# A two-layer MLP behind a recurrent scan: weight conversion with one POOL instruction less, and a scan whose decay is written straight into an operand

## The chip, the cores and the metric

One core of a Trainium2 chip runs the whole program. The metric is the device time of one execution in microseconds (us), taken in separate runs; the profile is one more execution, recorded by the hardware. The engines are TensorE (PE; its weight loads are PEld), VectorE (DVE), ScalarE (ACT), GpSimd (POOL) and SyncE (SP), which issues nearly all DMAs. Each engine takes its instructions strictly in the order written down for it and waits on semaphores for the others.

## What is computed

A linear recurrence over 768 time steps for 4 batches of 8 heads of width 40, and then two gated MLPs on the 3072 resulting rows of 320 (cut to what matters):

```
y[t] = r[t] @ state
Sa = state @ a[t]
state = state * w[t] - outer(Sa, b[t]) + outer(v[t], k[t])
...
h = x @ w_in;  x = (max(h, 0) + alpha * min(h, 0)) @ w_out
x = (silu(x @ w_gate) * (x @ w_val)) @ w_out2
```

The MLP weights come as 8-byte floats: w_in 320x2048, w_out 2048x320, w_gate and w_val 320x1536, w_out2 1536x320.

## The kernel before, in words

**The scan.** Time is cut into blocks of 128 steps (six, counted by m) and each block into two segments of 64. For each block, `prep_a` and `prep_b` (L491, L524) form decay products (Wx, rest), the matrices AN and kbt and their products on PE; `inverse(m)` (L586) inverts all triangular 32x32 pieces of a block by 31 elimination steps, on DVE and, for block 0, partly on POOL (L617, L625), and ends with two DVE transposes, the second at L631; two rounds of small matmuls (L639, L658) complete it. Then `seq(i, ch)` (L675) runs one batch of one block; two channels ch run side by side, each with one PSUM bank (tag s0 or s1) that all its steps share. A seq has two scan steps c. A step starts with `decay` (L695: the state ST times Wx, DVE, L697), copies the decayed state into halves of the operand gs (DVE, L713; POOL fills the other halves from v at L706), transposes the state on PE (sp, L718), copies that to s on ACT (L720), and then makes the products zp (L725, from gs), pp, gp and yp. At its end DVE adds the new part to the state (L775) and writes the output piece (L779).

**The conversion.** `conv` (L196) loads one 128-row piece of 8-byte weights as pairs of 32-bit words (tile raw, two buffers) and `narrow` (L173) makes fp32 of it. Three DVE bit instructions fold the exponent and join sign, high and low bits: L179 (mask and shift the high word, into wy), L180 (add the sign, into wz), L181 (add three low bits, into wy). ACT then writes the absolute value of the high word, read as fp32, into wz (L182); POOL compares it with a least value (L188) and multiplies the 0 or 1 into wy's number (L189), so that too small numbers become 0. `split` (L192) makes a rounded head on ACT (L193) and the rest on POOL (L194). There is one buffer of wy (YB = 1) and there are two of wz (ZB = 2). 32 pieces of the first MLP and 12 of the second go back to DRAM (tensor wd) and are fetched again as wt; 24 more of the second are converted late and directly into place (`direct`, L921), and in every other one of those DVE does comparison and product in one instruction (L184). An issue rule keeps POOL's instruction at L188 behind the last elimination step that POOL was given.

**The order.** `drive` (L127) draws from generators (preparations, inverse, the two scan channels, conversions, the first MLP `mlp1` of the block before) at given rates, each with a priority, and a scheduler then writes a fixed order for each engine. So a changed instruction can move all others. The first MLP of block m - 1 runs beside the scan of block m; after the last block's first MLP the second MLP runs alone (L960 on), from 885 us.

Of the kernel before, what the change touches and what calls it, by code (L numbers as in the profile page):

```python
# [7 lines left out]
F32 = mybir.dt.float32  # L8
F32R = mybir.dt.float32r
U32 = mybir.dt.uint32  # L10
ACTF = mybir.ActivationFunctionType
ALU = mybir.AluOpType
# [27 lines left out]
ZB = 2  # L40
GD0 = 0
GD1 = 0
GD2 = 0
BGS = 0
# [7 lines left out]
YB = 1  # L52
# [17 lines left out]
L = 64  # L70
# [5 lines left out]
def kernel(  # L76
# [15 lines left out]
    nc = tc.nc  # L92
# [78 lines left out]
    LEAST = 1.125 * 2.0 ** -15  # L171

    def narrow(pool, raw, dve=0):  # L173
        whi, wlo = raw[..., 1], raw[..., 0]
        sh = list(whi.shape)
        y = pool.tile(sh, U32, tag="wy", name="wy", bufs=YB)
        z = pool.tile(sh, U32, tag="wz", name="wz", bufs=ZB)
        f = z.bitcast(F32)
        nc.vector.tensor_scalar(y, whi, 0x07FFFFFF, 3, ALU.bitwise_and, ALU.logical_shift_left)  # L179
        nc.vector.scalar_tensor_tensor(z, whi, 0xC0000000, y, ALU.bitwise_and, ALU.bitwise_or)  # L180
        nc.vector.scalar_tensor_tensor(y, wlo, 29, z, ALU.logical_shift_right, ALU.bitwise_or)  # L181
        nc.scalar.activation(out=f, in_=whi.bitcast(F32), func=ACTF.Abs)  # L182
        if dve:
            nc.vector.scalar_tensor_tensor(f, f, LEAST, y.bitcast(F32), ALU.is_ge, ALU.mult)  # L184
            return f
        gate = tc.issue_after(mark["pool"].ins) if "pool" in mark else nullcontext()
        with gate:
            nc.gpsimd.tensor_scalar(f, f, LEAST, None, ALU.is_ge)  # L188
        nc.gpsimd.tensor_tensor(out=f, in0=f, in1=y.bitcast(F32), op=ALU.mult)  # L189
# [6 lines left out]
    def conv(stage, idx, src, f, kind, into=None, dve=None):  # L196
# [10 lines left out]
        w32 = narrow(stage, raw, (GD0 <= idx < GD1 or idx < 2 * K1 and GD2 and idx % GD2 == 0) if dve is None else dve)  # L207
# [467 lines left out]
    def seq(i, ch, own=None):  # L675
# [19 lines left out]
        def decay(c):  # L695
            std = st[:, :, 0:D].rearrange("q (a j) d -> q a j d", j=2)
            nc.vector.tensor_tensor(  # L697
                out=std, in0=std, in1=wv_all[:, :, :, c, L:L + 1].to_broadcast([128, NP // 2, 2, D]), op=ALU.mult
            )

        decay(0)
        for c in range(CPB):
            cs = slice(c * L, c * L + L)
            gs = (gs_x if i < B and c == 0 and BGS else gs_p).tile([128, NP, 2, L + D], F32, tag="gs", name="gs")
# [7 lines left out]
            for h, pr in ((0, lo), (1, hi)):  # L712
                nc.vector.tensor_copy(  # L713
                    out=gs[pr, h::2, :, L:L + D], in_=st[pr, :, 0:D].rearrange("q (a j) d -> q a j d", j=2)
                )
# [60 lines left out]
            if c < CPB - 1:  # L776
                decay(c + 1)
# [272 lines left out]
```

## Time and profile before

| | us |
|---|---|
| three runs | 1284.64, 1289.05, 1291.42 (median 1289.05) |
| profiled execution, its own time | 1285.88 |
| its span | 1284.2 |
| PE busy | 1107.7 (86% of the span) |
| DVE busy | 797.8 (62%) |
| ACT busy | 594.4 (46%) |
| POOL busy | 378.7 (29%) |
| chain of work that ended last | PE 47%, DVE 17%, DMA 10%, ACT 6%, POOL 3% |
| granted PE clock, mean | 0.942 |

Busy shares are means over stages that differ: in the first tenth of the span DVE is busy 90% and more and PE a third, in the last third it is the other way. A wait is put down to the engine whose signal came last.

### The profile page before, as it was taken

The numbers are of one execution on the slowest core, as the hardware profiler recorded it, in microseconds if no ns is written. First come the engines' busy times: TensorE is split into PE (matmuls) and PEld (weight loads), VectorE is DVE, ScalarE is ACT, GpSimd is POOL, SyncE is SP. The second block draws the span as 40 slices with busy tenths as digits, with TensorE's granted clock in tenths as the row PEclk, the third lists the DMA queues.
The fourth block names the chain that finished last, engine by engine and source line by source line (L and its number), as shares of the span: only waits on it lengthen the run. The fifth ranks groups of instructions, "written<-read, shape, count | busy, mean of one in ns | idle before, by whom it ended". The sixth has DMA issues, their size and how long they took to land.

```text
span 1284.2 us, 24671 instructions
## 1 busy us (share of the span) xinstructions
PE 1107.7 (86%) x9056; PEld 933.6 (73%) x9056; DVE 797.8 (62%) x1725; ACT 594.4 (46%) x1463; POOL 378.7 (29%) x580
## 2 busy tenths in 40 slices
PE   3531778878898998989799989999999999999998
PEld 3431667766677786878677766777888888888887
DVE  6999778899669748975767447657532323232222
ACT  4741666644764575475465344435332323232222
POOL 9786666655320221232046004324200000000000
PEclk9765789989999998999999999999999999999999
DMA  5321368777545444564558567986210101000000
GB/s 156 123 66 46 125 197 277 262 241 227 179 129 174 138 127 142 150 191 117 154 175 255 152 205 248 302 292 205 66 46 1 45 1 36 2 11 11 11 11 21
DMA packets 94215, 170.70 MB, mean 133 GB/s; under 512 B 12944, under 2 KB 42896, under 8 KB 94096
## 3 DMA queue, kind: packets, MB, share of 16 engines
q1 hardware_dynamic: 85936, 165.20, 40.7%
q10 hardware_dynamic: 8160, 3.93, 1.1%
q8 instruction: 72, 1.18, 0.4%
q14 instruction: 47, 0.39, 0.1%
HBM read 141.30 MB, written 27.79 MB: 132 GB/s over the span
## 4 chain that ended last, share of the span: by engine, by line
PE 47%; DVE 17%; DMA 10%; ACT 6%; issue 4%; POOL 3%; SPq 1%; ACTq 0%; DVEq 0%; POOLq 0%
PE pg L238 10%; PE pv L238 10%; PE u L238 6%; DMA wt<-wd 4%; PE o L971 3%; PE o L970 3%; PE o L972 3%; DVE la L625 2%; DVE g L278 2%; DVE tmp L617 2%; PE mnp L543 2%; DMA xd<-pv 2%; PE gp L752 1%; DVE gl L194 1%; DVE wz L180 1%
## 5 line engine op out<-in xcount | busy, mean ns | idle before, releaser
L193 ACT CAST gh<-g 128x512 fp32r<-128x512 f32 (+1 forms) x176 | 105.8, 601 | 170.2 <-DVE g L986 121.4
L986 DVE TENSOR_TENSOR g<-pv,sg 128x512 f32<-128x512 f32 x72 | 49.8, 692 | 216.2 <-PE pv L238 215.3
L194 DVE TENSOR_TENSOR gl<-g,gh 128x512 fp32r<-128x512 f32 (+1 forms) x176 | 123.9, 704 | 76.5 <-ACT gh L193 75.7
L238 PE MATMUL u<-xh,wt 128*128 128x512 f32 (+1 forms) x416 | 148.6, 401 | 25.7 <-DVE g L278 18.4
L278 DVE SCALAR_TENSOR_TENSOR g<-g,neg,u 128x512 f32<-128x512 f32 (+1 forms) x104 | 72.8, 700 | 71.7 <-ACT g L277 71.3
L238 PEld LDWEIGHTS u<-xh,wt 128*128 128x128 f32 x416 | 79.1, 193 | 50.7 <-DVE g L278 26.6
L543 PE MATMUL mnp<-AN,kbt 128*128 128x128 f32 x384 | 66.9, 336 | 51.7 <-DVE AN L518 42.6
L984 ACT ACTIVATE sg<-pg 128x512 f32<-128x512 f32 x72 | 42.9, 598 | 134.9 <-PE pg L238 134.9
L188 POOL TENSOR_SCALAR wz<-wz 128x384 f32<-128x384 f32 (+1 forms) x56 | 67.5, 1206 | 123.0 <-ACT wz L182 60.4
L543 PEld LDWEIGHTS mnp<-AN,kbt 128*128 128x128 f32 x384 | 61.4, 243 | 56.5 <-issue 26.1
L238 PE MATMUL pg<-xh,w 128*128 128x512 f32 x288 | 101.8, 394 | 0.2 <-ACT sg L984 0.2
L238 PE MATMUL pv<-xh,w 128*128 128x512 f32 x288 | 100.5, 389 | 0.0
L277 ACT ACTIVATE g<-u 128x512 f32<-128x512 f32 (+1 forms) x104 | 58.7, 564 | 78.0 <-PE u L238 61.2
L971 PE MATMUL o<-w,gh 128*128 128x320 f32 x288 | 87.7, 309 | 0.0
L970 PE MATMUL o<-w,gh 128*128 128x320 f32 x288 | 87.2, 308 | 0.0
L625 DVE TENSOR_TENSOR la<-la,tmp 128x120 f32<-128x120 f32 (+37 forms) x304 | 84.7, 306 | 1.6
L244 PE MATMUL d<-gl,wt 128*128 128x512 f32 (+1 forms) x208 | 82.6, 400 | 3.0 <-DVE gl L194 2.8
L706 POOL COPY gs<-raw_v 64x160 f32<-64x160 f32 x96 | 37.7, 393 | 160.0 <-PE yp L767 56.3
L617 DVE TENSOR_TENSOR tmp<-la 128x120 f32<-128x120 f32 (+37 forms) x304 | 82.1, 298 | 1.3
L557 POOL TENSOR_SCALAR_AFFINE_SELECT AN<-AN 64x256 f32<-64x256 f32 x96 | 52.1, 543 | 103.1 <-ACT AN L556 65.9
L238 PE MATMUL u<-xl,wt 128*128 128x512 f32 (+1 forms) x208 | 80.7, 388 | 0.5 <-DVE xl L194 0.4
L245 PE MATMUL d<-gh,wt 128*128 128x512 f32 (+1 forms) x208 | 79.0, 382 | 0.0
(120 smaller groups left out, 2753.2 us busy)
## 6 DMA issues: line engine op xcount, KB each, us to landing
wt<-wd SPq DMA_DIRECT2D x104, 384.0 KB
wt<-wd SPq DMA_DIRECT2D x104, 320.0 KB
wd<-wc SPq DMA_DIRECT2D x24, 384.0 KB
raw<-in_moe_w_out_dram SPq DMA_DIRECT2D x28, 320.0 KB
raw_wa<-in_wa_dram SPq DMA_DIRECT2D x48, 160.0 KB
raw_bk<-in_bk_dram SPq DMA_DIRECT2D x48, 160.0 KB
wd<-wc SPq DMA_DIRECT2D x20, 320.0 KB
raw<-in_moe_w_in_dram SPq DMA_DIRECT2D x16, 256.0 KB
```

Source lines behind the costliest of these rows:

```text
L188: nc.gpsimd.tensor_scalar(f, f, LEAST, None, ALU.is_ge)
L193: nc.scalar.copy(out=h, in_=raw)
L194: eng.tensor_tensor(out=l, in0=raw, in1=h.bitcast(F32), op=ALU.subtract)
L238: nc.tensor.matmul(ps, lt, rh, start=(i == 0), stop=(i == len(ops) - 1))
L244: nc.tensor.matmul(ps, wh, gl, start=False, stop=False)
L245: nc.tensor.matmul(ps, wl, gh, start=False, stop=last)
L278: nc.vector.scalar_tensor_tensor(g, g, neg[:, f:f + 1], ps, ALU.mult, ALU.add)
L543: nc.tensor.matmul(ps[:, s].rearrange("p h t -> p (h t)"), kbt[:, g * SH + s].rearrange("p j t -> p (j t)"), an[:, :, g * SH + s, :],)
L617: eng.tensor_tensor(out=tv, in0=ml[:, r0:r1, kk:kk + 1].to_broadcast([128, nr, ns]), in1=tl[:, kk:kk + 1, c0:c1].to_broadcast([128, nr, ns ...
L625: last = eng.tensor_tensor(out=dst, in0=dst, in1=tv, op=ALU.subtract)
L970: nc.tensor.matmul(ops[q], gh[:, ts], wh, start=first, stop=False)
L971: nc.tensor.matmul(ops[q], gh[:, ts], wl, start=False, stop=False)
```

## The change

Conversion: ACT's absolute value is made first, POOL takes the maximum of it and 2^-15 in place, and the three DVE bit instructions then work in place on that tile (three buffers of wz, none of wy). A number at the least value becomes 0 in the mask and shift, so no product is needed; nor has `direct` a form of its own any more. The bit steps two and three still read raw.

Scan: DVE writes the decayed halves of the state as products straight into gs, for step c + 1 right behind the addition of step c. The state itself is decayed in place after that: on DVE for the second step, on POOL for the first.

```diff
-ZB = 2
+ZB = 3
-YB = 1
...
-    LEAST = 1.125 * 2.0 ** -15
+    LEAST = 2.0 ** -15
-    def narrow(pool, raw, dve=0):
+    def narrow(pool, raw):
         whi, wlo = raw[..., 1], raw[..., 0]
-        sh = list(whi.shape)
-        y = pool.tile(sh, U32, tag="wy", name="wy", bufs=YB)
-        z = pool.tile(sh, U32, tag="wz", name="wz", bufs=ZB)
-        f = z.bitcast(F32)
-        nc.vector.tensor_scalar(y, whi, 0x07FFFFFF, 3, ALU.bitwise_and, ALU.logical_shift_left)
-        nc.vector.scalar_tensor_tensor(z, whi, 0xC0000000, y, ALU.bitwise_and, ALU.bitwise_or)
-        nc.vector.scalar_tensor_tensor(y, wlo, 29, z, ALU.logical_shift_right, ALU.bitwise_or)
+        y = pool.tile(list(whi.shape), U32, tag="wz", name="wz", bufs=ZB)
+        f = y.bitcast(F32)
         nc.scalar.activation(out=f, in_=whi.bitcast(F32), func=ACTF.Abs)
-        if dve:
-            nc.vector.scalar_tensor_tensor(f, f, LEAST, y.bitcast(F32), ALU.is_ge, ALU.mult)
-            return f
         gate = tc.issue_after(mark["pool"].ins) if "pool" in mark else nullcontext()
         with gate:
-            nc.gpsimd.tensor_scalar(f, f, LEAST, None, ALU.is_ge)
-        nc.gpsimd.tensor_tensor(out=f, in0=f, in1=y.bitcast(F32), op=ALU.mult)
+            nc.gpsimd.tensor_scalar(f, f, LEAST, None, ALU.max)
+        nc.vector.tensor_scalar(y, y, 0x07FFFFFF, 3, ALU.bitwise_and, ALU.logical_shift_left)
+        nc.vector.scalar_tensor_tensor(y, whi, 0xC0000000, y, ALU.bitwise_and, ALU.bitwise_or)
+        nc.vector.scalar_tensor_tensor(y, wlo, 29, y, ALU.logical_shift_right, ALU.bitwise_or)
         return f
...
-        def decay(c):
-            std = st[:, :, 0:D].rearrange("q (a j) d -> q a j d", j=2)
-            nc.vector.tensor_tensor(
-                out=std, in0=std, in1=wv_all[:, :, :, c, L:L + 1].to_broadcast([128, NP // 2, 2, D]), op=ALU.mult
-            )
-        decay(0)
+        std = st[:, :, 0:D].rearrange("q (a j) d -> q a j d", j=2)
+        def decayed(eng, out, pr, c):
+            wc = wv_all[pr, :, :, c, L:L + 1].to_broadcast([pr.stop - pr.start, NP // 2, 2, D])
+            eng.tensor_tensor(out=out, in0=std[pr], in1=wc, op=ALU.mult)
+        def start(c):
+            t = gs_p.tile([128, NP, 2, L + D], F32, tag="gs", name="gs")
+            for h, pr in ((0, lo), (1, hi)):
+                decayed(nc.vector, t[pr, h::2, :, L:L + D], pr, c)
+            decayed(nc.vector if c else nc.gpsimd, std, slice(0, 128), c)
+            return t
+        nxt = start(0)
         for c in range(CPB):
...
-            gs = (gs_x if i < B and c == 0 and BGS else gs_p).tile([128, NP, 2, L + D], F32, tag="gs", name="gs")
+            gs = nxt
...
-            for h, pr in ((0, lo), (1, hi)):
-                nc.vector.tensor_copy(
-                    out=gs[pr, h::2, :, L:L + D], in_=st[pr, :, 0:D].rearrange("q (a j) d -> q a j d", j=2)
-                )
...
             if c < CPB - 1:
-                decay(c + 1)
+                nxt = start(c + 1)
```

In the orders below lines have their numbers of the kernel they belong to; in the changed one L179 is POOL's maximum, L180 to L182 are the bit steps, L187 is the rest of a split, L692 a product with the decay, L771 and L775 the addition to the state and the output piece.

DVE, the end of the first scan step of both channels, before (ST0 and ST1 are the states of two batches):

```order
L775 TENSOR_TENSOR ST0_176<-yp_1434,ST0_176 128x4x40
L779 TENSOR_TENSOR pv_1028<-yp_1434,Wx_203 128x2x2x64
L697 TENSOR_TENSOR ST0_176<-ST0_176,Wx_203 128x4x40
L713 COPY gs_1519<-ST0_176 64x2x2x40 x2
L775 TENSOR_TENSOR ST1_178<-yp_1450,ST1_178 128x4x40
L779 TENSOR_TENSOR pv_1033<-yp_1450,Wx_235 128x2x2x64
L697 TENSOR_TENSOR ST1_178<-ST1_178,Wx_235 128x4x40
L713 COPY gs_1530<-ST1_178 64x2x2x40 x2
L532 TENSOR_TENSOR kbt_2689<-raw_bk0_141,rest0_115 128x8x64 x2
```

and now:

```order
L771 TENSOR_TENSOR ST0_176<-yp_1402,ST0_176 128x4x40
L775 TENSOR_TENSOR pv_1016<-yp_1402,Wx_203 128x2x2x64
L692 TENSOR_TENSOR gs_1416<-ST0_176,Wx_203 64x2x2x40 x2
L692 TENSOR_TENSOR ST0_176<-ST0_176,Wx_203 128x4x40
L771 TENSOR_TENSOR ST1_178<-yp_1421,ST1_178 128x4x40
L775 TENSOR_TENSOR pv_1021<-yp_1421,Wx_233 128x2x2x64
L692 TENSOR_TENSOR gs_1435<-ST1_178,Wx_233 64x2x2x40 x2
L525 TENSOR_TENSOR kbt_2625<-raw_bk0_141,rest0_115 128x8x64 x2
L692 TENSOR_TENSOR ST1_178<-ST1_178,Wx_233 128x4x40
```

The state's own decay stood ahead of the two writes into gs and stands behind them now, for the second channel behind a kbt product too.

DVE, right behind that place, before (wy is the one buffer, raw the loaded words):

```order
L179 TENSOR_SCALAR wy_1224<-raw_1220 128x384
L180 SCALAR_TENSOR_TENSOR wz_1225<-raw_1220,wy_1224 128x384
L181 SCALAR_TENSOR_TENSOR wy_1224<-raw_1220,wz_1225 128x384
L179 TENSOR_SCALAR wy_1264<-raw_1262 128x320
L180 SCALAR_TENSOR_TENSOR wz_1265<-raw_1262,wy_1264 128x320
L181 SCALAR_TENSOR_TENSOR wy_1264<-raw_1262,wz_1265 128x320
L532 TENSOR_TENSOR kbt_2837<-raw_bk0_141,rest1_116 128x8x64 x2
```

and now:

```order
L180 TENSOR_SCALAR wz_1329<-wz_1329 128x320
L181 SCALAR_TENSOR_TENSOR wz_1329<-raw_1327,wz_1329 128x320
L182 SCALAR_TENSOR_TENSOR wz_1329<-raw_1327,wz_1329 128x320
L180 TENSOR_SCALAR wz_1363<-wz_1363 128x384
L181 SCALAR_TENSOR_TENSOR wz_1363<-raw_1359,wz_1363 128x384
L182 SCALAR_TENSOR_TENSOR wz_1363<-raw_1359,wz_1363 128x384
L180 TENSOR_SCALAR wz_1381<-wz_1381 128x320
L181 SCALAR_TENSOR_TENSOR wz_1381<-raw_1379,wz_1381 128x320
L182 SCALAR_TENSOR_TENSOR wz_1381<-raw_1379,wz_1381 128x320
L180 TENSOR_SCALAR wz_1444<-wz_1444 128x384
L181 SCALAR_TENSOR_TENSOR wz_1444<-raw_1440,wz_1444 128x384
L182 SCALAR_TENSOR_TENSOR wz_1444<-raw_1440,wz_1444 128x384
```

Where two conversions followed each other, four of the run stand here; a fifth follows them, and the first of the run stands just ahead of the scan rows above.

POOL, at the end of the first inverse, before (wc is the converted piece, wz_813 and the others are its numbers):

```order
L194 TENSOR_TENSOR wc_820<-wz_813,wc_820 128x256
L194 TENSOR_TENSOR wc_820<-wz_813,wc_820 128x64
L652 MEMSET tt0_174 32x32x32 x2
L188 TENSOR_SCALAR wz_1051<-wz_1051 128x384
L189 TENSOR_TENSOR wz_1051<-wz_1051,wy_1050 128x384
L194 TENSOR_TENSOR wc_1058<-wz_1051,wc_1058 128x384
```

and now:

```order
L179 TENSOR_SCALAR wz_1038<-wz_1038 128x384
L187 TENSOR_TENSOR wc_808<-wz_802,wc_808 128x256
L187 TENSOR_TENSOR wc_808<-wz_802,wc_808 128x64
L179 TENSOR_SCALAR wz_1065<-wz_1065 128x320
L187 TENSOR_TENSOR wc_1044<-wz_1038,wc_1044 128x384
L179 TENSOR_SCALAR wz_1124<-wz_1124 128x384
L645 MEMSET tt0_174 32x32x32 x2
```

The product is gone, and the maximum of the next conversion now stands ahead of the rest of the one before.

## Rows read from the trace of the kernel before

**Rows 1.** Busy time in five stages: bounds, length, PE, PEld, DVE, ACT, POOL.

```profile
0.00:128.00 128.00, 42.23 (x356) 39.21 (x356) 116.58 (x277) 56.81 (x160) 100.86 (x186) 0.71 0.32 98
128.00:320.00 192.00, 155.88 (x1923) 134.24 (x1925) 165.29 (x379) 113.19 (x327) 116.44 (x155) 0.88 0.69 221
320.00:740.00 420.00, 385.64 (x4124) 316.05 (x4118) 301.25 (x747) 244.17 (x650) 109.59 (x192) 0.97 0.53 161
740.00:885.00 145.00, 130.69 (x640) 99.16 (x639) 90.89 (x143) 66.56 (x129) 37.81 (x35) 1.00 0.80 259
885.00:1284.00 399.00, 393.22 (x2028) 344.91 (x2026) 123.81 (x183) 113.70 (x201) 13.99 (x13) 1.00 0.08 27
```

**Rows 2.** DVE in order of time: start us, us; end of the third inverse.

```profile
317.05 1.94 DVE L631 STREAM_TRANSPOSE tt<-la 128x1024 f32<-128x1024 f32 x1
```

**Rows 3.** DVE groups by line and shape: busy us, mean ns | idle before.

```profile
L194 DVE TENSOR_TENSOR gl<-g,gh 128x512 fp32r<-128x512 f32 x160 | 113.7, 711 | 72.9 <-ACT gh L193 72.2
L278 DVE SCALAR_TENSOR_TENSOR g<-g,neg,u 128x512 f32<-128x512 f32 x88 | 65.3, 742 | 70.4 <-ACT g L277 70.1
L713 DVE COPY gs<-ST 64x160 f32<-64x160 f32 x96 | 31.3, 326 | 5.3 <-PE yp L767 3.5
L181 DVE SCALAR_TENSOR_TENSOR wy<-raw,wz 128x320 uint32<-128x320 uint32 x28 | 18.1, 645 | 0.3
L180 DVE SCALAR_TENSOR_TENSOR wz<-raw,wy 128x320 uint32<-128x320 uint32 x28 | 17.8, 637 | 1.4 <-POOL w L194 0.7
L697 DVE TENSOR_TENSOR ST<-ST,Wx 128x160 f32<-128x160 f32 x48 | 16.9, 353 | 0.1
L179 DVE TENSOR_SCALAR wy<-raw 128x320 uint32<-128x320 uint32 x28 | 11.2, 400 | 15.8 <-POOL wz L189 15.7
L184 DVE SCALAR_TENSOR_TENSOR wz<-wz,wy 128x384 f32<-128x384 f32 x8 | 4.5, 558 | 0.9 <-ACT wz L182 0.9
```

**Rows 4.** The same view, POOL's and ACT's part of a conversion.

```profile
L188 POOL TENSOR_SCALAR wz<-wz 128x384 f32<-128x384 f32 x32 | 39.9, 1245 | 86.3 <-ACT wz L182 39.7 <-DMA wt<-wd 37.4 <-DVE g L278 5.5
L189 POOL TENSOR_TENSOR wz<-wz,wy 128x384 f32<-128x384 f32 x32 | 33.9, 1061 | 2.1
L182 ACT ACTIVATE wz<-raw 128x384 f32<-128x384 f32 x40 | 22.1, 554 | 43.4 <-DVE wy L181 34.7 <-issue 3.3 <-DMA wt<-wd 2.8
```

**Rows 5.** DVE's waits, 0 to 320, 530 to 720, 720 to 920: us, times, longest.

```profile
DVE wy L179 <- POOL wz L189: 8.1, 4, 4.2
...
DVE wy L179 <- POOL wz L189: 7.4, 4, 4.8
...
DVE wy L179 <- POOL wz L189: 10.1, 8, 3.0
```

**Rows 6.** Busy time by stage of line L189 alone: bounds, length, POOL.

```profile
0.00:128.00 128.00, 6.49 (x6) 0.71 0.32 98
128.00:320.00 192.00, 23.80 (x25) 0.88 0.69 221
320.00:740.00 420.00, 13.34 (x13) 0.97 0.53 161
```

**Rows 7.** DVE and POOL in order of time, 241 to 244 us.

```profile
242.23 0.68 DVE L755 TENSOR_TENSOR gs<-gp,mask 128x512 f32<-128x512 f32 x1
242.83 0.89 DVE L697 TENSOR_TENSOR ST<-ST,Wx 128x160 f32<-128x160 f32 x1
...
241.41 1.18 POOL L188 TENSOR_SCALAR wz<-wz 128x320 f32<-128x320 f32 x1 [0.91 <-ACT wz L182]
...
242.67 0.87 POOL L189 TENSOR_TENSOR wz<-wz,wy 128x320 f32<-128x320 f32 x1
```

**Rows 8.** The chain of work that ended last: start us, us; one load of raw.

```profile
198.30 2.94 DMA raw<-in_moe_w_in_dram
```

**Rows 9.** The same chain, eight matmuls of 512 columns in the second layer.

```profile
885.76 1.84 PE pg L238 x8
```

**Rows 10.** PE's waits: 530 to 720 for g, the whole span for s.

```profile
PE u L238 <- DVE g L278: 3.4, 2, 3.1
...
PE zp L725 <- ACT s L720: 10.2, 8, 2.4
```

More of the change, by code (lines that the diff above doesn't have):

```diff
@@ L194, in split, with conv @@
         eng.tensor_tensor(out=l, in0=raw, in1=h.bitcast(F32), op=ALU.subtract)
-    def conv(stage, idx, src, f, kind, into=None, dve=None):
+    def conv(stage, idx, src, f, kind, into=None):
         sw = words(src)
@@ L206, in conv @@
             nc.sync.dma_start(out=raw, in_=sw[f * 128:f * 128 + 128])
-        w32 = narrow(stage, raw, (GD0 <= idx < GD1 or idx < 2 * K1 and GD2 and idx % GD2 == 0) if dve is None else dve)
+        w32 = narrow(stage, raw)
         t = stage.tile([128, 768], F32R, tag="wc", name="wc", bufs=WCB) if into is None else into
@@ L925, in direct @@
                 t = wpool.tile([128, 768 if kind == "up" else 2 * DM], F32R, tag=f"w{j}", name=f"w{j}")
-                conv(tail, 2 * K1 + 3 * f + j, src, f, kind, t, (3 * f + j) % 2)
+                conv(tail, 2 * K1 + 3 * f + j, src, f, kind, t)
                 held[f] = t.rearrange("p (a b) -> p a b", a=6) if kind == "up" else t
```

## The prediction

> **What bounds the kernel now.** I read the stages first, then what VectorE (DVE) waits for, then prices by instruction. The table of stages [rows 1] has columns PE, PEld, DVE, ACT, POOL. Up to 128 us DVE is busy 116.6 of 128 and the tensor engine (PE) 42: the preparation of scan inputs and the first triangular inverse run on DVE. From 128 to 320 us DVE is busy 165.3 of 192, PE 155.9 at 0.88 of its clock. From 320 to 740 PE is busy 385.6 of 420 and DVE only 301.3. From 740 to 885, where the last first-layer MLP runs beside the direct conversions, PE is busy 130.7 of 145. From 885 on PE is busy 393.2 of 399, so nothing in this change can shorten that stretch. The kernel is thus DVE's until the third inverse ends at 317.05 + 1.94 = 319 us [rows 2], and PE's after that, with about 34 us of PE gaps in 320 to 740 and 14 in 740 to 885.
>
> The prices are in [rows 3] (DVE), [rows 4] (POOL), the waits in [rows 5].
>
> **The change, part by part, against the profiled execution's 1285.88 us** (the median of the three runs, 1289.05, is 3.2 above it).
>
> *The multiplication leaves POOL.* Each POOL conversion made a comparison (1.25 us at 128x384) and a product of two tensors (1.06 us) [rows 4]; now it makes one maximum, the same one-tensor form as the comparison. No row shows a maximum; the nearest bounds are the Abs on the same tile on ACT, 0.55 us, and the comparison, 1.25 us [rows 4]; I take 1.2. The product was on POOL for 6.5 us before 128 us and for 23.8 us from there to 320 [rows 6]. What matters is what it did to DVE: a state decay, 0.353 us in the mean, took 0.89 us while such a product ran from 242.67 to 243.54, and a 512-element mask just before it, beside the comparison, took its usual 0.68 [rows 7]. So 0.54 us of DVE are lost in the 0.71 us of company, three quarters of it, and the comparison costs nothing. 0.75 x 30.3 = 23 us if a two-input DVE instruction ran beside all of it. Against that stand the eight state decays that POOL now makes before 320 us, also products of two tensors: between 0.35 us (DVE's decay, [rows 3]) and 1.06 us (POOL's product) each, I take 0.5, so 8 x 0.5 x 0.75 = 3 us. DVE has gaps and one-input work too, so I take half of the rest, **-10 us** for DVE before the third inverse ends; ends 0 and -20.
>
> *The stalls behind one buffer.* Before, the bit steps wrote wy, of which there is one, so the first step of a conversion waits for POOL's product of the previous one: 8.1 us of idle DVE up to 320, 7.4 in 530 to 720, 10.1 after 720 [rows 5]. That wait has no reason left. In its place the first bit step waits for POOL's maximum of its own conversion, and the two raw buffers are now held until the third bit step, since that still reads them. In the new DVE order six conversions follow each other after the second scan step with nothing between. Raw buffer to next bit step is then one DMA (2.94 us), one Abs (0.55) and one maximum (1.2), 4.7 us [rows 4, 8], against the 0.40 + 0.64 + 0.65 = 1.7 us of the one conversion between [rows 3]: a stall of 3 us on two or three of them. So **0 up to 320 us** (-8.1 + 8; ends -8 and +8).
>
> *DVE's list ahead of the third inverse's end.* In the new order it holds 10 state decays fewer (10 x 0.353), one conversion more (1.7), two first-layer steps fewer (2 x (0.742 + 0.711) = 2.9, moved, not saved), and 32 half-height products in place of copies [rows 3]. Copies average 0.326 us and the decay of twice the partitions 0.353, so I price a product at 0.03 above a copy, 0.9 us for the 32, since a mean holds the waits that both forms meet beside POOL. The Trainium skill ("VectorE: DVE Perf Modes", perf-mode tier table) says that an fp32 copy within SBUF runs at two elements a cycle and a tensor_tensor at one, which speaks against this edit: by it each product would cost 80 cycles more, an estimate of 0.083 us, 2.7 us for those 32 and 8 for all 96 of the kernel. Sum -3.5 + 1.7 - 2.9 + 0.9 = **-3.8 us**.
>
> So the third inverse ends about 14 us earlier. But PE has done less by then: the 32 matmuls of those two steps come later, at 1.84 us for eight [rows 9] 7.4 us. After 320 PE is the bound, so they are paid: **-14 + 7.4 = -6.6 us** (by the ends above DVE moves by +4 to -32, so +12 to -24).
>
> *320 to 740.* DVE loses 7.4 us of stalls, sixteen decays (5.6 us) and 13.3 us of POOL products beside it. It isn't the bound there; PE is covered by its own queue and pays only where it waits for DVE: its longest such wait there, for the activation g, is 3.4 us in 530 to 720 [rows 10]. I take **-2 us**; 0 and -8 are the ends. *The scan's chain.* The products into gs now come ahead of the second step's decay on DVE, and PE's transposes of the state need the decayed state. The copy s of the transposes must then leave their PSUM bank before zp starts, the wait that PE shows: 10.2 us in 8 of 48 scan steps [rows 10]. So the path of every second step grows by two products, 0.7 us, twelve times per channel; where that is the path, one time in six, **+1.4 us** (0 to +8). The first step's decay goes to POOL, and its products stand on DVE a whole scan step ahead, so I cost it nothing; that cover is gone where POOL is late, at 0.5 us for each of 24.
>
> *740 to 885.* Twelve conversions that DVE finished itself with one product (0.56 us, [rows 3]) now use POOL's maximum; the 10.1 us of stalls go, and raw is held 1.2 us longer. PE's gaps of 14 us are shared among many causes. **-1 us**; ends -5 and +10. After 885 us nothing.
>
> Sum: -6.6 - 2 + 1.4 - 1 = -8.2, 1277.7 us on the profiled execution's scale, 1281 on the median's. I say **1280**.
>
> **The rivals.** *Nothing comes through.* From 320 us PE sets the end and its work is unchanged, so 7.4 us of postponed matmuls and the longer scan chain eat the 10 us of DVE. For it: PE's 92% in 320 to 740. Against: PE's 36 us of gaps in 128 to 320. Then 1289, with 1283 to 1294 around it. *All of it comes through.* The postponed steps fill gaps that PE has after 320 anyway (34 us), and DVE's 14 us and the 7.4 us of stalls arrive whole: 1289 - 14 - 7.4 = 1268. *Slower: DVE now queues behind POOL.* All engines run in order, and behind a first bit step that waits for a maximum stand the inverse, the scan and the first layer's activations. POOL's queue at that place holds subtractions of a previous conversion and the masks. A mean wait of 0.7 us over the 32 conversions before 320 (22 us) takes all that DVE gained there, 14 + 8.1. That is the deciding point: at a mean of 1.2 us, one maximum, DVE ends 16 us later than I say and the time is 1281 + 16 = 1297; at twice that it is over 1310. For it: today's waits of DVE for POOL last up to 4.8 us [rows 5], so the order that was written down is late by that much on the chip. Against: three buffers, where there was one.
>
> **How the numbers follow.** A measurement of this kernel tells about 0.5% (6.4 us) from no change: faster is below 1282.6, slower above 1295.5. My forecast (1273 to 1287) has 0.42, of which two thirds lie below 1282.6; all through 0.15; nothing 0.26; slower 0.17. Faster 0.28 + 0.16 = 0.44; slower 0.17 and the edge of nothing, 0.19; the same 0.37. The range takes in the gain at its far side and the slower case up to a mean wait of 1.3 us: 1264 to 1299.
>
> **What would show it.** Right: no DVE wait for a POOL product; the third inverse ending near 305 us; DVE's two-input steps near their times without company; the dense second layer starting at 877 in place of 885. Wrong: a wait of the first bit step for the maximum of over 20 us before 320; the third inverse no earlier than 317; SyncE waiting longer for raw buffers, and PE with gaps behind weights in 740 to 885.

## The result, and the profile after

The changed kernel took 1301.21 us (median of 4 runs, 1299.57 to 1304.8) against 1287.41 us (median of 4 runs of the kernel before, taken with them). The ratio is 1.0109, with a 95% interval of 1.0071 to 1.0146: slower by about 14 us, just outside the range, where I had forecast 8 us less. The profiled execution took 1299.57 us; its span is 1297.9.

The first four stages of the changed kernel, cut at the same times as [rows 1] (columns PE, PEld, DVE, ACT, POOL, granted clock, DMA share, GB/s):

```profile
0.00:128.00 128.00, 39.77 (x356) 36.51 (x356) 109.58 (x271) 58.74 (x164) 105.97 (x184) 0.71 0.35 104
128.00:320.00 192.00, 149.25 (x1958) 131.16 (x1958) 152.64 (x377) 114.32 (x330) 98.62 (x145) 0.86 0.70 217
320.00:740.00 420.00, 390.09 (x4054) 316.78 (x4054) 296.12 (x724) 240.63 (x643) 95.67 (x182) 0.97 0.53 160
740.00:885.00 145.00, 125.94 (x635) 94.80 (x635) 80.22 (x130) 62.55 (x124) 37.56 (x36) 1.00 0.78 250
```

Up to 320 us DVE is 19.7 us less busy than in [rows 1] (262.2 against 281.9), and PE has done 9 us less. From 740 to 885 all of them are less busy: PE by 4.8 us, DVE by 10.7. So the engines wait more there, all of them.

DVE's waits for POOL's maximum, in the three stretches of [rows 5]:

```profile
DVE wz L180 <- POOL wz L179: 26.2, 9, 8.1
...
DVE wz L180 <- POOL wz L179: 7.9, 4, 3.1
...
DVE wz L180 <- POOL wz L179: 8.0, 7, 4.5
```

Ahead of 320 us they are 18 us longer than those for the product were; later they are much the same (7.9 and 8.0 against 7.4 and 10.1). The end of the third inverse, which [rows 2] put at 319, is at 312.73 + 1.98 = 314.7 us:

```profile
312.73 1.98 DVE L624 STREAM_TRANSPOSE tt<-la 128x1024 f32<-128x1024 f32 x1
```

**Where the time went** is read from milestones of the two traces, with those of the runs that follow (us from the start of each span; "activation 80" is the end of the 80th DVE step of the first MLP's activation g; "late waits" are what ACT and DVE together wait for a load of raw from 780 to 900 us):

| kernel | third inverse ends | last state addition ends | activation 80 | first matmul of the second layer | span | late waits for raw |
|---|---|---|---|---|---|---|
| before | 319.0 | 754.5 | 785.7 | 885.6 | 1284.2 | 1.6 |
| changed | 314.7 | 759.3 | 785.8 | 896.8 | 1297.9 | 24.2 |
| conversion alone | 303.9 | 749.5 | 786.3 | 895.4 | 1295.3 | 20.7 |
| scan alone | 337.7 | 786.7 | 809.5 | 909.9 | 1308.5 | 4.1 |
| scan alone, DVE's decay | 331.3 | 779.8 | 782.9 | 887.1 | 1287.0 | 3.3 |
| changed, DVE's decay | 307.1 | 754.5 | 788.0 | 895.0 | 1294.9 | 26.9 |
| changed, old late conversions | 316.3 | 759.8 | 785.5 | 885.8 | 1284.4 | 0.9 |
| conversion alone, old late ones | 308.3 | 754.5 | 789.0 | 886.2 | 1285.1 | 0.0 |
| changed, third raw buffer late | 313.4 | 757.5 | 785.7 | 894.3 | 1293.4 | 13.5 |
| changed, late max on DVE | 314.8 | 759.3 | 785.1 | 892.1 | 1296.8 | 20.6 |
| changed, late Abs and max on DVE | 312.5 | 755.7 | 781.2 | 892.4 | 1294.5 | 12.4 |
| changed, two late wz | 316.6 | 764.8 | 791.9 | 896.2 | 1299.1 | 18.7 |
| changed, one late wz | 316.5 | 766.4 | 791.7 | 888.2 | 1286.6 | 1.3 |
| changed, one late wz, three raw | 316.0 | 761.3 | 786.6 | 883.1 | 1281.5 | 0.0 |
| before, three late wy and wz | 318.9 | 754.3 | 789.3 | 897.2 | 1299.2 | 9.3 |
| before, third raw buffer late | 321.0 | 754.5 | 784.9 | 888.7 | 1287.3 | 3.1 |
| conversion alone, one late wz, three raw | 305.3 | 751.5 | 784.6 | 878.5 | 1276.9 | 0.0 |
| changed, DVE's decay, one late wz, three raw | 310.9 | 760.3 | 789.4 | 886.9 | 1285.3 | 0.0 |

The expectations below give 752.9 for the last state addition of the kernel before, and 6.6 us by which the conversion alone ends it earlier. Those are times of the last addition but one; the last ends at 754.5, and 5.0 us earlier with the conversion alone.

The first two rows say it: at activation 80 the two kernels are level. All of the loss arises between 786 and 897 us, where the last first-layer MLP runs beside the 24 late direct conversions, and just behind it. Eight of these kernels have the same written order as the changed kernel up to the late conversions; their third inverse ends between 312.5 and 316.6, so 4 us between two executions say nothing there. Nor do 6 us at activation 80: it is at 785.8 in the changed kernel and at 791.9 with two late wz, whose order is the same up to 827 us. The stretch from activation 80 to the second layer says more: 99.9 us before, 111.0 now.

PE, PEld, DVE, ACT and POOL in that stretch, before and now:

```profile
786.00:886.00 100.00, 92.97 (x386) 70.86 (x386) 66.09 (x103) 44.64 (x82) 33.08 (x31) 1.00 0.83 276
```

```profile
786.00:886.00 100.00, 87.24 (x358) 65.62 (x359) 56.28 (x90) 40.62 (x77) 32.51 (x30) 1.00 0.80 266
```

ACT's waits of 780 to 900 us for a load of raw, SyncE's (its DMA queue's) for a raw buffer, and PE's for the activation g and its rounded head gh. Before:

```profile
ACT wz L182 <- DMA raw<-in_moe_w_val_dram: 1.4, 1, 1.4
...
SPq L201 <- ACT wz L182: 13.3, 9, 4.2
SPq L206 <- ACT wz L182: 5.6, 5, 1.9
...
PE u L238 <- DVE g L278: 1.6, 2, 1.0
```

And in the changed kernel:

```profile
ACT wz L176 <- DMA raw<-in_moe_w_gate_dram: 9.9, 4, 3.1
...
ACT wz L176 <- DMA raw<-in_moe_w_out_dram: 7.2, 7, 2.6
ACT wz L176 <- DMA raw<-in_moe_w_val_dram: 7.1, 4, 2.5
...
SPq L194 <- DVE wz L182: 18.5, 9, 4.5
SPq L199 <- DVE wz L182: 14.4, 6, 3.7
...
PE u L231 <- DVE g L271: 8.1, 8, 2.0
...
PE d L236 <- ACT gh L186: 2.0, 1, 2.0
...
PE pg L231 <- DVE g L271: 1.3, 1, 1.3
```

One turn of it, in order of time (start us, us; first SyncE's issues, then ACT, DVE, PE):

```profile
798.20 0.38 SPq L194 DMA_DIRECT2D raw<-in_moe_w_gate_dram  x1
...
799.14 1.11 SPq L196 DMA_DIRECT2D raw<-in_moe_w_gate_dram  x2
...
803.73 0.55 ACT L176 ACTIVATE wz<-raw 128x384 f32<-128x384 f32 x1 [3.14 <-DMA raw<-in_moe_w_gate_dram]
804.18 0.45 ACT L186 CAST w<-wz 128x320 fp32r<-128x320 f32 x1
804.53 0.59 ACT L270 ACTIVATE g<-u 128x512 f32<-128x512 f32 x1
...
805.15 0.75 DVE L271 SCALAR_TENSOR_TENSOR g<-g,neg,u 128x512 f32<-128x512 f32 x1 [3.44 <-ACT g L270]
...
805.95 0.50 PE L231 MATMUL u<-xh,wt 128*128 128x512 f32 x1 [2.00 <-DVE g L271]
```

The load is issued at 798.2, 0.1 us behind the third bit step that frees a raw buffer (797.55 + 0.55); ACT reaches the Abs of that conversion before the load has landed and stands 3.1 us. The first layer's activation g is behind the Abs in ACT's order, DVE's half of g behind ACT's, and PE, which needs the PSUM buffer of u that DVE's g frees, stands for 2.0 us. ACT stands for raw 15 times from 780 to 900 us, while the MLP makes 26 steps.

### The profile page after: what moved, and what is told of

It is laid out like the page before. It is cut to its first block, busy times and chain, and to the rows that moved or that the text cites. A ratio compares the mean times of both kernels' runs of the same rounds, so it can differ in the third digit from the quotient of the medians.

```text
span 1297.9 us, 24528 instructions
## 1 busy us (share of the span) xinstructions
PE 1108.1 (85%) x9056; PEld 930.7 (72%) x9056; DVE 766.1 (59%) x1689; ACT 592.4 (46%) x1463; POOL 353.6 (27%) x560
## 4 chain that ended last, share of the span: by engine, by line
PE 52%; DVE 18%; DMA 15%; ACT 5%; issue 4%; POOL 4%; SPq 1%; ACTq 0%; DVEq 0%; POOLq 0%
PE pg L231 10%; PE pv L231 10%; PE u L231 7%; PE o L967 3%; PE o L966 3%; PE o L968 3%; DMA wt<-wd 3%; DMA xa<-xd 2%; DVE rest L494 2%; DVE la L618 2%; DMA raw_wa<-in_wa_dram 2%; DMA xd<-pv 2%; PE d L236 2%; PE gp L748 2%; PE yp L763 2%
## 5 line engine op out<-in xcount | busy, mean ns | idle before, releaser
L187 DVE TENSOR_TENSOR gl<-g,gh 128x512 fp32r<-128x512 f32 (+1 forms) x176 | 119.4, 679 | 92.5 <-ACT gh L186 91.9
L179 POOL TENSOR_SCALAR wz<-wz 128x384 f32<-128x384 f32 (+1 forms) x68 | 81.8, 1204 | 109.9 <-ACT wz L176 66.0
L536 PE MATMUL mnp<-AN,kbt 128*128 128x128 f32 x384 | 62.6, 315 | 44.8 <-DVE AN L511 34.2
L536 PEld LDWEIGHTS mnp<-AN,kbt 128*128 128x128 f32 x384 | 56.5, 224 | 49.9 <-POOL la L584 16.4
L968 PE MATMUL o<-w,gl 128*128 128x320 f32 x288 | 76.7, 308 | 0.0
L618 DVE TENSOR_TENSOR la<-la,tmp 128x120 f32<-128x120 f32 (+42 forms) x304 | 75.0, 277 | 1.6
```

What stands on the lines that cost most here:

```text
L179: nc.gpsimd.tensor_scalar(f, f, LEAST, None, ALU.max)
L187: eng.tensor_tensor(out=l, in0=raw, in1=h.bitcast(F32), op=ALU.subtract)
L536: nc.tensor.matmul(ps[:, s].rearrange("p h t -> p (h t)"), kbt[:, g * SH + s].rearrange("p j t -> p (j t)"), an[:, :, g * SH + s, :],)
L618: last = eng.tensor_tensor(out=dst, in0=dst, in1=tv, op=ALU.subtract)
L968: nc.tensor.matmul(ops[q], gl[:, ts], wh, start=False, stop=last)
```

## The experiments

Ratios are those of the timed runs to runs of the kernel before on the same chip, with the 95% interval.

**One part alone.** The changed conversion with the scan of before, and the changed scan with the conversion of before:

```diff
-ZB = 2
+ZB = 3
...
+            nc.gpsimd.tensor_scalar(f, f, LEAST, None, ALU.max)
...
-                conv(tail, 2 * K1 + 3 * f + j, src, f, kind, t, (3 * f + j) % 2)
+                conv(tail, 2 * K1 + 3 * f + j, src, f, kind, t)
```

> The conversion is that of the changed kernel (three buffers, POOL's maximum first, also in the late direct conversions), the scan that of the kernel before. Theory A (the loss is made between 786 and 897 us by the direct conversions: the raw buffers are held until the third bit step, so raw is loaded late, ScalarE's Abs waits for it, 24 us in the changed kernel against 1.4 before, and the first layer's activation stands behind that Abs): 1297 to 1304 us, like the changed kernel, the second layer's first matmul 8 to 12 us later than the 885.6 of before, ScalarE waiting 15 us or more for raw after 780. Theory C (the scan part or its new order costs it): 1283 to 1291 and a second layer that starts at 885 +- 3. On the first stage: if the conversion gives the 4 us that the third inverse gained, it ends near 315 here; if the scan part gave them, near 319.

```diff
-        decay(0)
+        nxt = start(0)
...
-                decay(c + 1)
+                nxt = start(c + 1)
```

> The scan is that of the changed kernel, the conversion that of the kernel before, direct ones too. Theory A (the direct conversions cost it): 1284 to 1291 us, second layer from 882 to 889. Theory C (the scan part or its new order): 1297 to 1304, second layer from 893 on. Scan chain as I priced it (+1.4 us, 0 to +8): the last state addition between 752 and 761 against 752.9.

The conversion alone: 1298.47 us, ratio 1.0098 (1.0067 to 1.0129), the whole loss, although its third inverse ends 15.1 us earlier than before. The scan alone: 1309.9 us, 1.0169 (1.0127 to 1.0211), outside what theory A allowed and of another kind: it is late by 18.8 us at the third inverse and by 23.8 at activation 80, and by no more than that at the second layer (24.3). Up to activation 80 PE is busy 638.4 us there, for the same 6648 matmul records that take 622.2 in the kernel before; the granted clock in that stretch is 0.88 in the mean against 0.91. Why the clock was lower is not shown. Each part thus costs something by itself, in another place, and the two don't add: the changed kernel is faster than the scan alone.

**The old form for the late conversions only.** In the changed kernel and in the conversion alone:

```diff
+        w32 = narrow(stage, raw) if dve is None else narrow0(stage, raw, dve)
...
+                conv(tail, 2 * K1 + 3 * f + j, src, f, kind, t, (3 * f + j) % 2)
```

(narrow0 is the narrow of before, with one buffer of wy and two of wz.)

> The changed kernel, but the 24 late direct conversions are made as before (bit steps first, then Abs, every other one finished by VectorE, the others by POOL's comparison and product). Theory A: nearly all of the loss goes, 1286 to 1292 us, second layer from 883 to 889. Theory B (the loss comes from what the changed kernel does before 786 us, and shows only after it): 1298 to 1304, second layer from 894 on. Theory C (scan): as B.

> The changed conversion for the 44 early pieces, the old one for the 24 late ones, and the scan of before. In the run with the conversion alone the third inverse ended 15 us and the last scan step 6.6 us earlier, but the first layer's activation 80 at 786.3, as before. Theory P (the tensor engine's own work sets the end by then, so that an early gain is not worth anything): 1284 to 1289 us, ratio within 0.4% of 1, second layer at 885 +- 2. Theory Q (the early gain was there and the late conversions ate it): 1272 to 1281.

1286.53 us, ratio 1.0001 (0.9977 to 1.0025), and 1287.74 us, 0.9994 (0.9975 to 1.0013). The late conversions hold all of the loss. And the second one says what the early gain is worth beside the old ones: nothing that can be measured, though its third inverse ends 10.7 us earlier than in the kernel before.

**What is it about the late conversions?** I first took it for the raw buffers, which are held until the third bit step, then for POOL's place in the chain, then for ACT's. Three edits of the late conversions alone:

```diff
-            raw = stage.tile([128, 3, 128, 2], U32, tag="raw", name="raw", bufs=RB)
+            raw = stage.tile([128, 3, 128, 2], U32, tag="raw", name="raw", bufs=RB if into is None else 3)
```

> The changed kernel, with three raw buffers in place of two in the late direct conversions and nothing else. Theory A (raw is held too long): SyncE's waits of 33 us for the third bit step fall under 12, ScalarE's waits for raw from 24 to under 8, the second layer starts 6 to 11 us earlier than 896.8 and the time is 1288 to 1295 us. Rival A2 (in the direct conversions it is the wait for POOL's maximum, or the maximum's place in POOL's order, that delays VectorE's activations): no change, 1298 to 1304 us, though SyncE waits less.

```diff
+        if late:
+            nc.scalar.activation(out=f, in_=whi.bitcast(F32), func=ACTF.Abs)
+            nc.vector.tensor_scalar(f, f, LEAST, None, ALU.max)
```

> The changed kernel, but in the 24 late direct conversions VectorE takes the maximum, so that POOL is out of the chain ahead of the bit steps; the Abs stays first on ScalarE. Theory A2 (the loss of 11 us is the hop over POOL: 1.2 us of maximum and two hand-overs between the Abs and the bit steps, in a chain behind which ScalarE's head of the split and the first layer's activation stand): most of it goes, second layer from 885 to 890, 1286 to 1293 us. Rival A3 (it is the Abs at the head of ScalarE's queue, which waits for the load of raw, 24 us, wherever the maximum is made): second layer from 893 to 898, 1297 to 1303. Rival A1 (raw held too long) has been given 2.5 us by the third raw buffer; by it this one would gain 1 to 3 us.

```diff
+        if late:
+            nc.vector.tensor_scalar(y, whi, 0x7FFFFFFF, None, ALU.bitwise_and)
+            nc.vector.tensor_scalar(f, f, LEAST, None, ALU.max)
```

> As the one before, and the Abs is made by VectorE as a mask of the sign bit, so that neither ScalarE nor POOL stands between the load and the bit steps; five VectorE instructions a conversion in place of three (24 x 2 x about 0.4 = 19 us more of VectorE in a stage where it idles a third of the time). A3 (ScalarE's Abs waiting for raw): second layer from 884 to 890, 1285 to 1293 us, against no gain in the run with the maximum alone on VectorE. A2 (POOL's hop): like that run. If VectorE's added work decides: later than 893.

Ratios 1.0099 (1.0067 to 1.0132), 1.0098 (1.0076 to 1.012) and 1.0106 (1.0073 to 1.0139): all three theories fell in the form I had given them. The third raw buffer took 2.5 us from the start of the second layer and halved the late waits for raw, SyncE's waits for the third bit step fell from 33 us to 22 and not under 12, and the time did not move. With POOL out of the chain the second layer starts 4.7 us earlier and loses 3.6 of it at once: ACT stands for raw three times more (2.4, 0.9 and 0.5 us) ahead of the second layer's first sg, PE stands 3.3 us for that sg, and the granted clock is 0.50 in 905 to 910 us. So it isn't the hop alone. With ACT out of it too, DVE stands for the loads (12.4 us), and g is behind DVE's mask; how much of that loss is DVE's added work is not shown. What all three keep is that an engine's queue stands for raw.

**The number of buffers.** The kernel before had one buffer of wy, for which its first bit step waited; the change has three of wz, so that nothing but raw holds a conversion back. One and two buffers of wz for the late conversions, one with three of raw, and the opposite, the kernel before with three of wy and wz there (zb, and yb below, hold for the late conversions alone; the others keep their numbers):

```diff
-        y = pool.tile(list(whi.shape), U32, tag="wz", name="wz", bufs=ZB)
+        y = pool.tile(list(whi.shape), U32, tag="wz", name="wz", bufs=zb)
...
+        w32 = narrow(stage, raw, ZB if into is None else 1)
```

> The changed kernel, but with one buffer of wz in place of three for the 24 late conversions. Theory D (the one buffer of before paced the late conversions: the next one could not begin until POOL had finished the last, so that its raw words had long landed when the first reader's turn came; with three buffers the written order puts the first reader of raw, ahead of the first layer's activation, right at the end of a load that itself waits for a raw buffer): one buffer brings the pace back, ScalarE's waits for raw fall from 24 us to under 8, the second layer starts from 884 to 891 and the time is 1284 to 1294 us. Rival E (the new chain is simply too long in series, or too much is asked of VectorE between two activations): fewer buffers change nothing or cost more, 1297 to 1312 us.

> As the one before with two buffers of wz. Theory D: between one and three, 1288 to 1299 us. Rival E: 1297 to 1305.

> One buffer of wz and three of raw for the late conversions. Theory D: loads now run a whole conversion further ahead; ScalarE's wait for raw under 3 us, 1283 to 1292 us, second layer from 883 to 889. Rival E: as with three raw buffers alone, 1296 to 1304.

```diff
-        y = pool.tile(sh, U32, tag="wy", name="wy", bufs=YB)
-        z = pool.tile(sh, U32, tag="wz", name="wz", bufs=ZB)
+        y = pool.tile(sh, U32, tag="wy", name="wy", bufs=yb)
+        z = pool.tile(sh, U32, tag="wz", name="wz", bufs=zb)
```

> The kernel before, with its own conversion and its own scan, but three buffers each of wy and wz for the 24 late conversions in place of one and two. Theory D: the pace is gone and so is its protection; some engine waits for raw 10 us or more after 780 (VectorE's first bit step now, 0 before), the second layer starts from 889 to 898 and the time is 1291 to 1302 us though only buffers were added. Rival E (the new chain's form costs it): no change or a gain, 1280 to 1289.

| late conversions | us | ratio (95%) |
|---|---|---|
| changed, wz 3 (the change) | 1301.21 | 1.0109 (1.0071 to 1.0146) |
| changed, wz 2 | 1299.6 | 1.0095 (1.0067 to 1.0124) |
| changed, wz 1 | 1283.2 | 0.9971 (0.9948 to 0.9994) |
| changed, wz 1, raw 3 | 1281.57 | 0.9970 (0.9942 to 0.9998) |
| before, wy 3, wz 3 | 1300.09 | 1.0113 (1.0089 to 1.0136) |

Theory D holds in both directions for the number of buffers. With one buffer the changed kernel loses nothing; with more buffers and not one operation changed the kernel before loses as much as by the change. The stretch from activation 80 to the second layer is 96.5 us with one wz, 104.3 with two and 107.9 in the kernel before with three. (Two are as bad as three, by 0.6 us outside what I had allowed.) In the run with one buffer (SyncE, ACT):

```profile
798.37 0.38 SPq L194 DMA_DIRECT2D raw<-in_moe_w_val_dram  x1
798.81 0.47 SPq L196 DMA_DIRECT2D raw<-in_moe_w_val_dram  x1
...
799.96 0.48 SPq L196 DMA_DIRECT2D raw<-in_moe_w_val_dram  x1
...
805.53 0.54 ACT L176 ACTIVATE wz<-raw 128x384 f32<-128x384 f32 x1
...
810.93 0.50 ACT L176 ACTIVATE wz<-raw 128x320 f32<-128x320 f32 x1 [0.18 <-POOL w L187]
```

The load is issued at 798.4 to 800.4 and read at 805.5 without a wait: one more conversion lies between, since its Abs needs the wz that POOL's rest of the split (L187) frees, the wait in the last row. A conversion still waits, but for POOL and with its raw words landed, and hardly for a load (1.3 us in 780 to 900). PE in the same 100 us as above, in this run:

```profile
786.00:886.00 100.00, 94.48 (x402) 74.24 (x401) 55.65 (x96) 45.49 (x82) 29.40 (x28) 1.00 0.88 282
```

In the kernel before with three buffers DVE's first bit step stands for raw, which it did for 0.2 us before, and PE for g:

```profile
DVE wy L179 <- DMA raw<-in_moe_w_val_dram: 4.4, 5, 2.3
DVE wy L179 <- DMA raw<-in_moe_w_gate_dram: 3.7, 3, 1.8
DVE wy L179 <- DMA raw<-in_moe_w_out_dram: 1.3, 1, 1.3
...
PE u L238 <- DVE g L278: 10.6, 7, 2.8
```

Beside it, the kernel before with three raw buffers and its own one wy:

> The kernel before with three raw buffers for the late conversions and nothing else. If its paced conversions already had their raw words in time (VectorE waited 0.2 us for raw after 780), a third buffer is worth 0 to 3 us: 1282 to 1288, ratio 0.996 to 1.001. If more buffers of any kind loosen the order: 1291 or more.

1286.3 us, 0.9994 (0.9972 to 1.0016): as the first of the two had it.

One thing stays open. The number of buffers also changes the order that the scheduler writes. In the traces DVE and ACT keep to the order of the kernel before throughout when only a third raw buffer is added; with three of wy and wz they leave it at 775 us, where a conversion's first bit step moves ahead of an activation. The order of the changed kernel with one wz leaves that of the change from 780 us on. No run adds buffers and holds the order, so the runs show that the buffers make the loss, and not how much of it they make through the order alone.

**The scan part and the front.**

```diff
-            decayed(nc.vector if c else nc.gpsimd, std, slice(0, 128), c)
+            decayed(nc.vector, std, slice(0, 128), c)
```

In the changed kernel, and in the scan alone:

> The changed kernel, but the decay of the state for the first scan step is made by VectorE in place of POOL. The scan part moved the third inverse 10.8 us later beside the new conversion (303.9 to 314.7) and 18.8 later beside the old one. If that is POOL's decay (late on POOL, and a two-tensor product beside VectorE): the third inverse ends from 303 to 309 here. If it is the products in place of copies, or their place ahead of the transposes: 313 to 320. The time is that of the changed kernel either way, 1297 to 1304, since the late conversions are unchanged.

> The scan part alone, as in the second run, but with VectorE's decay in the first scan step too; nothing of the scan is left on POOL that was not there before. If POOL's decay makes the loss: the third inverse ends from 317 to 325 us (337.7 with it), VectorE's waits for POOL's product before 340 us fall from 23.7 to under 14, 1284 to 1294 us. If the products and their place make it: third inverse from 331 to 340, 1300 to 1312 us.

The changed kernel so: 1298.31 us, 1.0093 (1.0063 to 1.0123), third inverse at 307.1. POOL's decay thus makes 7.6 of the 10.8 us by which the scan part delays the third inverse beside the new conversion (by another pair of executions, 316.0 and 310.9, it is 5; by the means over the executions with the same order so far, 315.1 of eight, 309.0 of two and 305.8 of three, it is 6 of 9). The scan alone so: 1287.39 us, 0.9997 (0.9971 to 1.0024), and DVE's waits for POOL's product up to 340 us are 8.3 us in place of 18.9 (the 23.7 in the expectation has the longest single wait, 4.8, added to the total). The time is that of the first theory, the third inverse at 331.3 that of the second: it ends 12 us late and the last state addition even 25.3 us late, and the end does not move.

**With the late conversions paced.**

> The changed conversion with the scan of before, the late conversions paced by one buffer of wz and given three of raw. Theory P (up to 786 us the tensor engine's own work sets the pace, so that the 15 us by which the third inverse ends earlier are worth nothing): the same as with the changed scan and the same late conversions, ratio 0.994 to 1.000, 1279 to 1286 us. Theory Q (the early gain comes through once the late loss is gone): 1265 to 1276, ratio under 0.992.

> The changed kernel with VectorE's decay in the first scan step and the late conversions paced as in the run before. Theory P: ratio 0.994 to 1.000. Theory Q: third inverse near 307 and 5 to 8 us faster than with POOL's decay, ratio 0.989 to 0.993.

The conversion alone with one late wz and three raw: 1278.32 us, ratio 0.9943 (0.9921 to 0.9965), the fastest version of all, by 0.6% of the kernel before and 1.8% of the changed one (median against median). It is at the near edge of theory P, the ratio inside its range and the time 0.7 us below it: of the 10.7 us by which its third inverse ends ahead of that with the changed scan (305.3 against 316.0, ratio 0.9970), 3 us come through, between the medians, and the two intervals overlap. The second: 1281.63 us, 0.9967 (0.9951 to 0.9983), the same as with POOL's decay. PE in the 100 us of the first:

```profile
786.00:886.00 100.00, 97.00 (x413) 76.55 (x412) 52.06 (x90) 44.51 (x81) 28.60 (x27) 1.00 0.84 272
```

## Why the prediction was wrong

**The step that failed** is "740 to 885: ... the 10.1 us of stalls go, and raw is held 1.2 us longer. ... -1 us; ends -5 and +10", and the sentence on which it stands, "That wait has no reason left". For this -1 the runs have +11.2 us, by which the second layer starts later, and 2.5 us more go behind that. I took DVE's wait for the one buffer [rows 5] for a cost. In the late stage the one buffer was what kept a conversion from starting until the loads were ahead of it: three there cost the kernel before 1.0113, and one gives the change 0.9971. I did name the sign under "wrong" (SyncE waiting longer for raw, PE with gaps behind weights), and the first half came: 33 us of SyncE's waits against 19. But PE's gaps are behind g and its rounded head gh (11.4 us, 1.6 before) and not behind weights, since the queue that stood was ACT's, with the Abs as the first reader of raw, and not SyncE's alone. My upper end of +10 was made for the 1.2 us of longer holding; the third raw buffer, which answers to that, is worth 2.5 us at the start of the second layer and nothing that can be measured in the time.

**The POOL product leaves, -10 us for DVE:** not shown by itself. DVE is 19.7 us less busy up to 320 us, and the list below accounts for 3.8 of it by my sum; the other 16 are more than the 10 and inside its ends, but no run takes the product alone away. One reading under it was wrong: the mask of [rows 7] says nothing on the comparison, since the same step took 0.69 us at 213.80 beside a two-tensor subtraction on POOL too (213.12, 1.51 us). **The stalls, 0 up to 320 us:** wrong by 18 us: 26.2 us of waits for the maximum against 8.1. That is above the 22 us that I set as the deciding point of the slower rival. With the conversion alone, and in the change with DVE's decay, they are

```profile
DVE wz L181 <- POOL wz L180: 16.3, 11, 3.7
...
DVE wz L180 <- POOL wz L179: 13.8, 8, 5.1
```

so 10 of the 18 us come with the scan part, and 12 go when DVE makes its decay. **DVE's list, -3.8:** its piece on the products was too low. A product takes 370 ns against a copy's 326 [rows 3] in the mean, 44 above it and not 30. The means hold the steps that POOL stretched, and the copies more (their mean is 85 ns above their median, that of the products 48); by the medians (least, median and longest, ns) a product takes 81 ns more, 2.6 us for the 32 and not 0.9:

```profile
L713 DVE COPY gs<-ST x96: 207/241/1422, 31.7 to 739.7; 64x160 f32<-64x160 f32 x96
...
L692 DVE TENSOR_TENSOR gs<-ST,Wx x96: 304/322/1120, 28.1 to 742.7; 64x160 f32<-64x160 f32 x96
```

The mean of the products, in the view of [rows 3]:

```profile
L692 DVE TENSOR_TENSOR gs<-ST,Wx 64x160 f32<-64x160 f32 x96 | 35.5, 370 | 1.6 <-PE yp L763 0.7
```

The rule of the Trainium skill ("VectorE: DVE Perf Modes", perf-mode tier table) spoke for a larger difference than mine, 83 ns by my estimate from it; the medians agree with it. POOL's maximum takes 1237 ns, as the comparison did (1.2 in the sum), and POOL's decay 624 (0.5 in the sum):

```profile
L179 POOL TENSOR_SCALAR wz<-wz 128x384 f32<-128x384 f32 x40 | 49.5, 1237 | 87.8 <-ACT wz L176 49.7 <-DMA raw<-in_moe_w_val_dram 35.6 <-DMA wt<-wd 1.8
...
L692 POOL TENSOR_TENSOR ST<-ST,Wx 128x160 f32<-128x160 f32 x24 | 14.9, 624 | 10.1 <-DVE gs L692 9.7 <-PE yp L763 0.3
```

**The third inverse 14 us earlier:** 4.3 in the change, 15.1 with the conversion alone. The mechanism was there, and the scan part took seven tenths of it back, half or more of that by POOL's decay, which I had costed at nothing but for "0.5 us for each of 24" where POOL is late.

**-14 + 7.4 = -6.6, and -2 for 320 to 740:** wrong. It was worth nothing. (The 3.4 us under the -2 are two waits together; the longest is 3.1 [rows 10].) The rival "nothing comes through" had this half right: with the old late conversions the change is at 1.0001, and at 0.9994 without the scan part. The scan alone with DVE's decay shows it most sharply: the scan may end 25.3 us late without a loss. PE then does the first MLP's steps earlier: 79 of the first 80 are done when the last state addition ends, 73 in the kernel before. What is the same is PE's work up to activation 80: 6648 matmul records in the kernel before, the change, the conversion alone and the scan with DVE's decay, busy between 618.7 and 622.2 us. That this work sets the pace there is argued from these rows and not shown by a run of its own; PE stands idle 161 to 167 us ahead of activation 80 in each of them.

**The scan's chain, +1.4:** not settled. The last state addition ends at 759.3 against 754.5. From the third inverse to it the change takes 444.6 us, 1 us less than the conversion alone (445.6), but the scan alone takes 449.0 against 435.5 before, more than my upper end of +8. The scan end that was 25.3 us late, above, had no effect on the time.

**The slower rival** gave 1297, close to 1301, by another mechanism, so its number is right by luck. Its condition came true (26.2 us of waits) and DVE's third inverse ended 10 us later than the 305 I forecast, but that price was not paid: beside the same scan, the old late conversions alone bring the time back to 1.0001, and a third inverse 12 us later than before cost nothing in the scan with DVE's decay. In the scan alone, with a third inverse 18.8 us late, 24 us were lost, part of them at a lower clock; so how late it may be is open.

## What to carry to other kernels

A wait behind a scarce buffer may be what keeps loads ahead of their readers; before it is removed, see which wait ends the chain next, and on whose queue: a wait for a DMA in an engine's queue ahead of the bound engine's feeder was worse here than a wait for another engine elsewhere. An operation priced rightly and a stage made shorter were worth little here, where the kernels were level again at a later milestone, so predict at milestones. When a change brings buffers and operations together, try the buffers alone on the old kernel, and look whether the written order moved with them.

## What the runs showed of the hardware

A one-input DVE step is stretched by POOL's two-tensor work too, not only the two-input step of [rows 7]. In the kernel before two copies of the state into gs took 1.16 us beside POOL's product, where the median of one is 0.24; a state decay just ahead of them, beside POOL's comparison, took 0.31 us, its usual time:

```profile
190.85 0.31 DVE L697 TENSOR_TENSOR ST<-ST,Wx 128x160 f32<-128x160 f32 x1
...
191.69 1.16 DVE L713 COPY gs<-ST 64x160 f32<-64x160 f32 x2
...
190.52 1.00 POOL L188 TENSOR_SCALAR wz<-wz 128x320 f32<-128x320 f32 x1
191.61 0.87 POOL L189 TENSOR_TENSOR wz<-wz,wy 128x320 f32<-128x320 f32 x1
```

The same holds for the bit steps. DVE's first bit step now follows POOL's maximum, and POOL can then be at the rest of a split. The step took 0.84 us beside it (start us, us; DVE, then POOL), and 0.36 alone ten microseconds later:

```profile
810.51 0.84 DVE L180 TENSOR_SCALAR wz<-wz 128x384 uint32<-128x384 uint32 x1
...
820.59 0.36 DVE L180 TENSOR_SCALAR wz<-wz 128x384 uint32<-128x384 uint32 x1
...
810.13 1.00 POOL L187 TENSOR_TENSOR w<-wz,w 128x384 fp32r<-128x384 f32 x1
```

The mean of that step at 128x384 is 579 ns against 399 for its forerunner, which read raw and stood elsewhere in the order. The Trainium skill ("GPSIMD Engine Reference", 1. Specifications) names, as those that contend with GpSimd for the SBUF interfaces, DVE instructions with two inputs and those in a mode that uses both ports. The steps stretched here have one input and would fit the second kind; no row names the mode of a step.

PE's clock fell behind the last stops of the late stage. PE stood for 2.0 us up to 892.6 and again for 1.3 up to 896.8; the granted clock was 0.87 in the mean of 890 to 895 us, 0.50 in the next five (1.2 GHz, the lower level) and 0.95 in the five after:

```profile
890.00:895.00 5.00, 2.98 (x11) 1.84 (x9) 2.89 (x5) 1.14 (x3) 1.57 (x2) 0.87 0.58 175
895.00:900.00 5.00, 3.71 (x10) 2.57 (x9) 3.79 (x6) 2.63 (x6) 3.58 (x3) 0.50 0.24 66
900.00:905.00 5.00, 5.00 (x22) 4.08 (x21) 1.99 (x3) 1.13 (x3) 2.16 (x2) 0.95 0.50 146
```

The first eight matmuls of the second layer took 3.78 us in place of the 1.84 of [rows 9], 1.9 of the 2.5 us that the change lost behind that start:

```profile
896.79 3.78 PE pg L231 x8
```
